# Attention and MLP in one launch: the order of loads and first steps in the opening

## The chip, the cores and the metric

The kernel runs on one core of one Trainium2 chip. The core has a matrix engine (TensorE, PE in the profile, with its weight loads shown apart as PEld), a vector engine (DVE), a scalar engine (ACT), a general engine (POOL) and SyncE (SP), which here issues every DMA transfer. Each engine works through its own list of instructions in the order in which they stand there, and waits where an operand or a buffer is not ready. The metric is the device time of one execution in microseconds (us). Times are compared as the median of several executions.

## The reference

The input x has 2048 tokens of width 512. It is normalised per token, and the normalised tokens go through an attention with 32 query heads that share one head of keys and values (head width 16), and through a two-layer MLP of width 1792 with the Mish activation. The output is x plus both results. Cut to what matters:

```python
xn = (x - mean(x)) / sqrt(var(x) + 1e-5)               # 2048 x 512
q  = (xn @ wq) split into 32 heads of 16
k, v = xn @ wk, xn @ wv                                # one head of 16 each
p  = softmax(q @ k.T * 16**-0.5)                       # 32 x 2048 x 2048
A  = (p @ v for all heads, joined) @ wo
h  = xn @ w1 + b1
B  = (h * tanh(softplus(h))) @ w2                      # Mish, width 1792
out = x + A + B
```

Everything is float32. Products are made with a split of each operand into a high part and the remainder, three terms of four, so every matrix needs a rounded copy (hi) and a difference (lo) before it is used.

## The kernel before, in words

The work has two parts. The **opening** (the block under `with tc.tile_pool(name="first", ...)`) takes some 100 us. It loads the tokens in four chunks of 512 (chunk c is four tiles of 128 tokens), normalises them, transposes them on PE, and projects them to keys, values and queries. It also makes the first two tiles of the MLP (`hidden(0)`, `hidden(1)`) and the row maxima of the scores of the first four heads. The **main part** then follows a long string, `PLAN`, that fixes the order of scores, exponentials, values, MLP products and loads, one letter per step. The change does not touch this string.

In the opening the order on every engine is the order in which the Python code issues instructions: nothing is reordered. Some instructions are put off with `later(...)` and issued by a `flush(...)` of their tag. The functions that matter here, with the names that the profile shows:

- `load_tokens(c)` issues four DMAs into tiles `pt` (L314). `statistics(c)` makes mean and variance of each tile on DVE (L322, L323). `rooted(c)` puts variance and mean into `v` and `m` (DVE, L329, L330) and has ACT make the first guess of 1/sqrt by Ln and Exp (L331, L332). `root(c, engine)` improves it by a Newton step (L337 to L340). `normalise` and `normalise_on_two` scale the tiles (DVE or POOL L346, ACT L354).
- `first_transposes` and `transposes` turn the tiles on PE (L361, L375); ACT copies the result out of PSUM as the hi part of `X` (L363, L377), and DVE or POOL subtract for the lo part (L387).
- `keys_values(c)` multiplies `X` by `wkv` (PE L412); ACT copies the result twice (L417, L418), and POOL makes 16 rows of differences in `KS`. `queries(c, mt)` and `hidden(f)` are generators whose 12 products are issued by `Piece.product` (PE L703) in portions, wherever the code calls `fill_slot`. ACT copies a query block out (L448, L449), POOL makes its lo part (L452), SP sends it on (L458 to L475).
- `query_block(mt)` and `request("w1", f, ...)` load weights into a raw tile (`raw_block`, L257); `split` makes hi on ACT (L240) and lo on POOL (L241). Raw tiles are a ring of three (`RAWS`), shared by the query blocks and the MLP's blocks.
- `first_maxima` makes scores of the first heads (PE L490) into a pair of banks and takes their maxima on DVE (L507).

PSUM has eight banks. Three pairs rotate (`pair_bank`), bank 6 is called `o`, bank 7 `misc`. The first MLP tile, the second one and the query blocks of chunk 0 all use bank 7:

```python
p = bank("o", f"q{c}_{mt}", 1) if beside == [] and turn[0] % 2 else misc(f"q{c}_{mt}")
p = misc(f"h0_{f}")
```

`beside` holds the transposes and projections of chunks 2 and 3 and becomes empty only after they have been issued, so until then a query block may begin only when ACT has copied out the tile that was in bank 7 before.

SP's list is one queue too. A load that waits for a raw tile holds back everything behind it, including the copies of the first query block into `QS` (L469), which the first scores need.

Of the kernel before, what the change touches and what calls it, by code (L numbers as in the profile page):

```python
# [17 lines left out]
P = 128  # L18
# [16 lines left out]
WARM = 54  # L35
# [143 lines left out]
def attention_and_mlp(ctx: ExitStack, tc: tile.TileContext, x, wq, wk, wv, wo, w1, b1, w2, out):  # L179
# [73 lines left out]
    def raw_block(kind, i):  # L253
        raw = work.tile([P, D], F32, tag="raw", name=f"raw_{kind}{i}", bufs=RAWS)
# [61 lines left out]
    def statistics(c, some=range(NT)):  # L316
# [7 lines left out]
        if len(some) == NT:  # L324
            rooted(c)

    def rooted(c):
        v, y, z, m = (first.tile([P, NT], F32, tag=n, name=f"{n}{c}", bufs=2) for n in ("v", "y", "z", "m"))
        DVE.tensor_scalar_add(v, MV[c][:, :, 1], EPS)  # L329
        DVE.tensor_scalar_mul(m, MV[c][:, :, 0], -1.0)  # L330
        ACT.activation(z, v, AF.Ln)  # L331
        ACT.activation(y, z, AF.Exp, scale=-0.5)  # L332
        ROOT[c] = v, y, z, m

    def root(c, engine):
        v, y, z, m = ROOT[c]
        engine.tensor_tensor(out=z, in0=y, in1=y, op=ALU.mult)  # L337
# [10 lines left out]
    def normalise_on_two(c, n):  # L348
        v, y, z, mean = ROOT[c]
        DVE.tensor_tensor(out=z, in0=y, in1=mean, op=ALU.mult)  # L350
        normalise(c, DVE, range(n))
# [298 lines left out]
    def hidden(f):  # L650
# [3 lines left out]
        p = misc(f"h0_{f}")  # L654
# [80 lines left out]
    with tc.tile_pool(name="first", bufs=1) as first:  # L735
# [6 lines left out]
        request("w1", 0, WB[0])  # L742
# [7 lines left out]
        SP.dma_start(out=b1s, in_=b1.rearrange("(f p) -> p f", p=P))  # L750
# [9 lines left out]
        wkv = first.tile([P, 2, DT, P], F32R, name="wkv")  # L760
        for r in (0, 64):
# [8 lines left out]
        statistics(0)  # L770
        request("w1", 1, WB[1])
        ask()
        root(0, DVE)
        normalise_on_two(0, 2)
        WQ[1] = query_block(1)
        load_tokens(2)
        for mt in range(2, DT):
            WQ[mt] = query_block(mt)
        load_tokens(3)
        urgent += [queries(*divmod(i, DT)) for i in range(1, NC * DT)]  # L780
        ask()
# [324 lines left out]
```

## Time and profile before

| | |
|---|---|
| Median of 3 runs | 1553.24 us (1551.15 to 3630.99) |
| Profiled execution, its time | 1553.4 us |
| Profiled execution, its span | 1551.4 us |
| Mean granted PE clock | 0.999 |
| PE busy, DVE, ACT, POOL | 1539.8, 1346.6, 1343.8, 862.9 us |
| First product of queries and keys of chunk 0 | 12.80 us |
| First scores of the first heads | 32.01 us |
| First scores of the main part | 100.40 us |

The run of 3630.99 us stands far from the other two, which are 2.1 us apart. The span runs from the first to the last instruction; the time has about 2 us around it. In rows of the timeline the two numbers ahead are the start and the length in us, then come engine, line, operation, output and inputs, the number of instructions that a row merges, and in square brackets how long the engine had stood idle before it and what ended that.

### The profile page before, as it was taken

How to read it: one execution, taken by the hardware profiler on the slowest of the kernel's cores; microseconds unless marked ns; L12 is line 12 of the kernel's file. 1: busy time of each engine (PE TensorE's matmuls, PEld its weight loads, DVE VectorE, ACT ScalarE, POOL GpSimd, SP SyncE). 2: the span in 40 equal slices, each digit the busy share in tenths (PEclk: the TensorE clock that was granted, in tenths of full speed). 3: DMA queues.
4: the chain of work that ended last, by engine and by line, in shares of the span. 5: the costliest groups of instructions: out<-in, count | busy, mean ns of one | idle time of the engine just before them, and what ended most of it. 6: DMA issues, size and time to landing. Idle time of an engine off the chain costs nothing.

```text
span 1551.4 us, 30232 instructions
## 1 busy us (share of the span) xinstructions
PE 1539.8 (99%) x11554; PEld 847.3 (55%) x11554; DVE 1346.6 (87%) x2284; ACT 1343.8 (87%) x2388; POOL 862.9 (56%) x757
## 2 busy tenths in 40 slices
PE   8999999999999999999999999999999999999998
PEld 6665554555555555555555545555555555555555
DVE  6869998898999898999889999999988998999841
ACT  5569988999999889898889888988898989888896
POOL 5768765676565546544554474833374746353652
PEclk9999999999999999999999999999999999999999
DMA  6783322242122321125322321132222222142120
GB/s 187 279 301 113 107 85 87 82 141 105 60 66 87 119 73 60 45 72 173 80 73 93 112 90 43 51 124 103 86 94 79 86 78 80 32 127 94 43 96 29
DMA packets 69399, 152.53 MB, mean 98 GB/s; under 512 B 12774, under 2 KB 22054, under 8 KB 68870
## 3 DMA queue, kind: packets, MB, share of 16 engines
q1 hardware_dynamic: 69254, 150.60, 29.8%
q8 instruction: 91, 1.49, 0.4%
q14 instruction: 54, 0.44, 0.1%
HBM read 98.51 MB, written 51.64 MB: 97 GB/s over the span
## 4 chain that ended last, share of the span: by engine, by line
PE 96%; DMA 1%; DVE 0%; ACT 0%; issue 0%; SPq 0%; POOL 0%; ACTq 0%; POOLq 0%; DVEq 0%
PE banks L560 32%; PE banks L934 24%; PE banks L556 18%; PE banks L490 18%; PE banks L703 3%; DMA ring<-w_dram 1%; PE banks L642 1%; PE banks L412 0%; DMA wkv_raw<-in_A_wv_dram 0%; DMA pt<-in_A_x_dram 0%; PE banks L375 0%; DVE ysb L632 0%; POOL wblk L241 0%; SPq L314 0%; DVE X L387 0%
## 5 line engine op out<-in xcount | busy, mean ns | idle before, releaser
L502 DVE TENSOR_REDUCE nm<-banks 128x1 f32<-128x512 f32 x1984 | 1241.1, 683 | 126.1 <-PE banks L490 75.9
L999 ACT ACTIVATE pt<-banks 128x512 f32<-128x512 f32 x1590 | 858.3, 604 | 105.6 <-PE banks L556 51.5
L490 PE MATMUL banks<-KS,QS 48*128 48x512 f32 x2048 | 694.6, 421 | 0.0
L556 PE MATMUL banks<-QS,KS 64*128 64x512 f32 x2048 | 681.5, 418 | 0.0
L560 PE MATMUL banks<-pt,V 128*32 128x512 f32 x4096 | 536.2, 603 | 0.0
L556 PEld LDWEIGHTS banks<-QS,KS 64*128 64x128 f32 x2048 | 330.9, 184 | 224.7 <-DVE nm L502 106.5
L490 PEld LDWEIGHTS banks<-KS,QS 48*128 48x128 f32 x2048 | 334.1, 185 | 195.7 <-DVE nm L502 99.8
L934 PE MATMUL banks<-X,wblk 64*128 64x512 f32 x1296 | 330.9, 396 | 0.5
L934 PE MATMUL banks<-ring,act 64*128 64x512 f32 x1344 | 328.4, 396 | 0.8 <-DMA ring<-w_dram 0.6
L991 ACT ACTIVATE pt<-banks 128x1024 f32<-128x1024 f32 x229 | 233.1, 1029 | 34.6 <-PE banks L556 21.0
L934 PEld LDWEIGHTS banks<-X,wblk 64*128 64x128 f32 x1296 | 215.1, 185 | 31.5 <-issue 15.4
L934 PEld LDWEIGHTS banks<-ring,act 64*128 64x128 f32 x1344 | 212.3, 185 | 36.4 <-issue 10.3
L560 PEld LDWEIGHTS banks<-pt,V 128*32 128x32 f32 x4096 | 85.8, 108 | 176.7 <-issue 166.0
L945 POOL TENSOR_TENSOR ysb<-ysb,ty 128x512 f32<-128x512 f32 x80 | 102.7, 1285 | 122.7 <-ACT ty L944 122.1
L683 POOL TENSOR_TENSOR tn<-tn,tr 128x512 f32<-128x512 f32 x54 | 69.3, 1284 | 139.1 <-ACT tr L1009 139.0
L1004 POOL TENSOR_SCALAR tu<-tu 128x512 f32<-128x512 f32 x54 | 80.3, 1487 | 119.1 <-ACT tu L1003 118.8
L241 POOL TENSOR_TENSOR act<-th,act 128x512 fp32r<-128x512 f32 x56 | 72.0, 1288 | 128.3 <-ACT act L240 106.9
L686 POOL TENSOR_TENSOR th<-th,tn 128x512 f32<-128x512 f32 x56 | 72.3, 1291 | 0.0
L685 POOL TENSOR_TENSOR tz<-tz,tn 128x512 f32<-128x512 f32 x54 | 69.5, 1287 | 4.5
L1006 POOL TENSOR_TENSOR tn<-tn,tu 128x512 f32<-128x512 f32 x54 | 69.5, 1287 | 4.5
L687 POOL TENSOR_TENSOR th<-th,tz 128x512 f32<-128x512 f32 x54 | 69.5, 1287 | 4.2
L934 PE MATMUL banks<-ring,ohl 64*128 64x512 f32 x288 | 65.5, 397 | 0.0
(116 smaller groups left out, 960.2 us busy)
## 6 DMA issues: line engine op xcount, KB each, us to landing
wblk<-w_dram SPq DMA_DIRECT2D x42, 512.0 KB
ring<-w_dram SPq DMA_DIRECT2D x42, 512.0 KB
QS<-q_dram SPq DMA_DIRECT2D x62, 192.0 KB
q_dram<-q SPq DMA_DIRECT2D x16, 512.0 KB
o_dram<-ov SPq DMA_DIRECT2D x31, 256.0 KB
raw_w<-in_B_w_dram SPq DMA_DIRECT2D x28, 256.0 KB
w_dram<-wblk SPq DMA_DIRECT2D x14, 512.0 KB
w_dram<-ring SPq DMA_DIRECT2D x14, 512.0 KB
```

Of the source, the lines that this page charges most:

```text
L241: POOL.tensor_tensor(out=lo, in0=src, in1=hi.bitcast(F32), op=ALU.subtract)
L490: PE.matmul(tile, QS[u][rows, pair, qt * P : (qt + 1) * P], KS[rows, kc * CT : (kc + 1) * CT], start=True, stop=True,)
L502: DVE.tensor_reduce(out=m[:, a : a + 1], in_=tile, axis=AX.X, op=ALU.max)
L556: PE.matmul(bank, KS[rows, kt * P : (kt + 1) * P], QS[u][rows, pair], start=True, stop=True)
L560: PE.matmul(BANK[7][h * 32 : (h + 1) * 32], V[:, kt], PT.pop((u * KT + kt) * HG + h), start=kt == 0, stop=kt == KT - 1,)
L685: POOL.tensor_tensor(out=z, in0=z, in1=n, op=ALU.subtract)
L686: POOL.tensor_tensor(out=h, in0=h, in1=n, op=ALU.mult)
L934: PE.matmul(self.p, w[rows], x[rows], start=self.first, stop=not any(self.todo))
L945: POOL.tensor_tensor(out=YS[t], in0=YS[t], in1=ty, op=ALU.add)
L991: ACT.activation(slots[slot // 2], banks[:, bank : bank + 2], AF.Exp, scale=SCALE)
L999: ACT.activation(PT[n], BANK[bank], AF.Exp, scale=SCALE)
L1004: POOL.tensor_scalar_min(tu, tu, U_MAX)
```

## The change

Six things are altered, all in the opening:

- The raw tiles of query blocks 1 to 3 are no longer taken from the ring of three. They lie in tiles that the MLP uses later (`TN[0]`, `TN[1]`, `TH[2]`; `tn` and `th` in the order below).
- All loads of the opening are issued at its beginning, in the order MLP block 0, bias, MLP block 1, chunk 2, query blocks 1 and 2, chunk 3, query block 3.
- The statistics, the root and the scaling of chunk 0 are done in two halves of two tiles; POOL makes the Newton step of the first half. The split of `wkv` is divided: keys ahead of the second half's root, values behind the scaling.
- The Newton step is one instruction shorter on DVE, and the bias of ACT's scaling is made only for ACT's columns.
- The first MLP tile goes to bank 6.
- Some steps of chunks 1 to 3 trade places: the second MLP block is split earlier, `rooted(2)` and chunk 1's lo parts come ahead of the statistics of chunk 3, and two of these move behind the first two maxima. PE's first 54 transposes of the identity become 44.

```diff
-WARM = 54
+WARM = 44
@@ raw_block
-        raw = work.tile([P, D], F32, tag="raw", name=f"raw_{kind}{i}", bufs=RAWS)
+        if kind == "wq" and i:
+            raw = (TN + TH[2:])[i - 1]
+        else:
+            raw = work.tile([P, D], F32, tag="raw", name=f"raw_{kind}{i}", bufs=RAWS)
@@ rooted, root
-        DVE.tensor_scalar_add(v, MV[c][:, :, 1], EPS)
+        DVE.tensor_scalar(v, MV[c][:, some, 1], EPS, -0.5, op0=ALU.add, op1=ALU.mult)
-        ACT.activation(z, v, AF.Ln)
+        ACT.activation(z, v, AF.Ln, scale=-2.0)
...
-        engine.tensor_scalar(z, z, -0.5, 1.5, op0=ALU.mult, op1=ALU.add)
-        engine.tensor_tensor(out=y, in0=y, in1=z, op=ALU.mult)
+        if engine is DVE:
+            DVE.scalar_tensor_tensor(out=y, in0=z, scalar=1.5, in1=y, op0=ALU.add, op1=ALU.mult)
+        else:
+            engine.tensor_scalar_add(z, z, 1.5)
+            engine.tensor_tensor(out=y, in0=y, in1=z, op=ALU.mult)
@@ first_transposes
-        for t in (0, 2, 1, 3):
+        for t in range(NT):
@@ hidden
-        p = misc(f"h0_{f}")
+        p = misc(f"h0_{f}") if f else bank("o", f"h0_{f}", 1)
@@ opening
         load_tokens(1)
-        request("w1", 0, WB[0])
+        for f in range(2):
+            request("w1", f, WB[f])
+            ask()
+            if f == 0:
+                SP.dma_start(out=b1s, in_=b1_column)
+        load_tokens(2)
+        for mt in range(1, DT - 1):
+            WQ[mt] = query_block(mt)
+        load_tokens(3)
+        WQ[DT - 1] = query_block(DT - 1)
...
+        statistics(0, range(2))
+        rooted(0, halves[0])
+        root(0, POOL, halves[0])
         for r in (0, 64):
             hi, lo = (wkv[:, i, :, r : r + 48].rearrange("p t (k d) -> p t k d", k=3) for i in range(2))
             split(hi, lo, wkv_raw[:, :, None, :DH].to_broadcast([P, DT, 3, DH]))
-            split(wkv[:, 0, :, r + 48 : r + 64], wkv[:, 1, :, r + 48 : r + 64], wkv_raw[:, :, DH:])
-        statistics(0)
...
+        statistics(0, range(2, NT))
+        rooted(0, halves[1])
+        normalise(0, DVE, range(2))
+        root(0, DVE, halves[1])
+        normalise_on_two(0, 3, 2)
+        for r in (0, 64):
+            split(wkv[:, 0, :, r + 48 : r + 64], wkv[:, 1, :, r + 48 : r + 64], wkv_raw[:, :, DH:])
...
+        split_block()
         statistics(1, range(2))
...
-        split_block()
         flush(("k", 0))
         flush(("wq", 1), ("wq", 2))
+        statistics(2)
         fill_slot(12)
         run(transposes(1))
-        flush(("wq", 3))
-        statistics(2)
+        rooted(2)
+        flush(("lo", 1))
         statistics(3, range(2))
-        flush(("lo", 1))
         fill_slot(12)
         root(2, POOL)
         normalise(2, POOL)
-        statistics(3, range(2, NT))
         run(keys_values(1))
+        flush(("wq", 3))
...
             if i == 1:
+                statistics(3, range(2, NT))
                 rooted(3)
```

How this moves instructions is seen best engine by engine. On SP, the stretch between the second MLP block and the copies of the first query block reads before (`pt_82`, `pt_83` are the tiles of chunk 2, `pt_84`, `pt_85` those of chunk 3, two tiles each; the brackets name the semaphores waited for):

```order
L257 DMA raw_w_205<-in_B_w_dram 128x4x128 [waits DMAHW5_49]
L257 DMA raw_wq_217<-in_A_wq_dram 128x4x128 [waits DMAHW6_49,Pool_49]
L314 DMA pt_82<-in_A_x_dram 128x512 [waits DMAHW7_49]
...
L257 DMA raw_wq_224<-in_A_wq_dram 128x4x128 [waits DMAHW3_49,Pool_49]
L257 DMA raw_wq_227<-in_A_wq_dram 128x4x128 [waits DMAHW5_49,DMAHW4_49,Pool_49]
L314 DMA pt_84<-in_A_x_dram 128x512
...
L469 DMA QS_88<-q_0_307 16x2x512 [waits DMAHW1_49]
```

and after:

```order
L260 DMA raw_w_113<-in_B_w_dram 128x4x128 [waits DMAHW5_49]
L317 DMA pt_82<-in_A_x_dram 128x512 [waits DMAHW6_49]
...
L260 DMA tn_76<-in_A_wq_dram 128x4x128 [waits DMAHW2_49]
L260 DMA tn_77<-in_A_wq_dram 128x4x128 [waits DMAHW3_49]
L317 DMA pt_84<-in_A_x_dram 128x512 [waits DMAHW4_49]
...
L260 DMA th_75<-in_A_wq_dram 128x4x128 [waits DMAHW0_49]
L474 DMA QS_88<-q_0_303 16x2x512 [waits DMAHW1_49,Activation_49]
```

(Three dots stand for the chunk's other tiles.) The three loads of query blocks waited for POOL to release a raw tile, and wait now only for earlier transfers.

On DVE, from the last values of chunk 2 to the root of chunk 3, before (`st_398` are the statistics of chunk 3, `X_357` is the transposed chunk 1, `nm` the maxima):

```order
L330 TENSOR_SCALAR m_393<-mv_381 128x4
L322 BN_STATS st_398<-pt_84 128x6
L323 BN_AGGR mv_399<-st_398 128x2
...
L387 TENSOR_TENSOR X_357<-banks,X_357 128x1024 x2
L322 BN_STATS st_398<-pt_85 128x6
L323 BN_AGGR mv_399<-st_398 128x2
...
L507 TENSOR_REDUCE nm_451<-banks 128x2 x2
L329 TENSOR_SCALAR v_460<-mv_399 128x4
```

and after (`X_360` is the transposed chunk 1, `st_389` the statistics of chunk 3):

```order
L333 TENSOR_SCALAR m_382<-mv_335 128x4
L392 TENSOR_TENSOR X_360<-banks,X_360 128x1024 x2
L325 BN_STATS st_389<-pt_84 128x6
L326 BN_AGGR mv_390<-st_389 128x2
...
L512 TENSOR_REDUCE nm_440<-banks 128x2 x2
L325 BN_STATS st_389<-pt_85 128x6
L326 BN_AGGR mv_390<-st_389 128x2
...
L332 TENSOR_SCALAR v_453<-mv_390 128x4
```

The lo parts of chunk 1 moved ahead of the first two statistics of chunk 3, and the first two maxima ahead of the other two. (Where three dots stand, the same rows follow for the next tile of the chunk.) On ACT the copy of query block 1 out of PSUM stands behind Ln and Exp of chunk 3's root in both kernels; after the change these rows read:

```order
L423 ACTIVATE KS<-kvs_431 128x512
L240 ACTIVATE wq_127<-th_75 128x256 x2
L334 ACTIVATE z_455<-v_453 128x4
L335 ACTIVATE y_454<-z_455 128x4
L453 ACTIVATE q_1_473<-banks 128x512
```

Here the split of query block 3 has moved in from an earlier place on ACT; the three rows below it stand as before.

More of the change, by code (lines that the diff above doesn't have):

```diff
@@ L323, in statistics, with rooted, root @@
             DVE.bn_aggr(out=MV[c][:, t], in_=st[:, t])
[L324 to L328, printed above, removed]
[L329 to L331 removed]
+    def rooted(c, some=slice(0, NT)):
+        if c not in ROOT:
+            ROOT[c] = [first.tile([P, NT], F32, tag=n, name=f"{n}{c}", bufs=2) for n in ("v", "y", "z", "m")]
+        v, y, z, m = (t[:, some] for t in ROOT[c])
+        DVE.tensor_scalar(v, MV[c][:, some, 1], EPS, -0.5, op0=ALU.add, op1=ALU.mult)
+        DVE.tensor_scalar_mul(m, MV[c][:, some, 0], -1.0)
+        ACT.activation(z, v, AF.Ln, scale=-2.0)
         ACT.activation(y, z, AF.Exp, scale=-0.5)
[L333 to L336 removed]
+    def root(c, engine, some=slice(0, NT)):
+        v, y, z, m = (t[:, some] for t in ROOT[c])
         engine.tensor_tensor(out=z, in0=y, in1=y, op=ALU.mult)
         engine.tensor_tensor(out=z, in0=z, in1=v, op=ALU.mult)
[L339 to L340 removed]
+        if engine is DVE:
[3 more added lines that the diff above has]
+            engine.tensor_tensor(out=y, in0=y, in1=z, op=ALU.mult)
     def normalise(c, engine, some=range(NT)):
@@ L346, in normalise, with normalise_on_two @@
             engine.tensor_scalar(x, x, m, r, op0=ALU.add, op1=ALU.mult)
-    def normalise_on_two(c, n):
+    def normalise_on_two(c, n, begin=0):
         v, y, z, mean = ROOT[c]
-        DVE.tensor_tensor(out=z, in0=y, in1=mean, op=ALU.mult)
-        normalise(c, DVE, range(n))
+        DVE.tensor_tensor(out=z[:, n:], in0=y[:, n:], in1=mean[:, n:], op=ALU.mult)
+        normalise(c, DVE, range(begin, n))
         for t in range(n, NT):
@@ L768, in run @@
                 pass
-        statistics(0)
[L771 to L781, printed above, removed]
         flush(("wq", 0))
```

4 lines of the change are left out of this document (3 added, 1 removed).

## The prediction

> **What bounds the kernel now.** I read the page's totals and chain first.
>
> ```profile
> PE 1539.8 (99%) x11554; PEld 847.3 (55%) x11554; DVE 1346.6 (87%) x2284; ACT 1343.8 (87%) x2388; POOL 862.9 (56%) x757
> PE 96%; DMA 1%; DVE 0%; ACT 0%; issue 0%; SPq 0%; POOL 0%; ACTq 0%; POOLq 0%; DVEq 0%
> ```
>
> PE is the bound, and its list behind the opening is untouched. So the change is worth what it moves PE's list forward by the end of the opening, and that carries to the end undiminished. Next I read PE's timeline over the opening:
>
> ```profile
> 1.35 7.73 PE L747 MATMUL banks<-ident 128*128 128x128 f32 x54 [1.35 <-POOL ident masks.py:199]
> 12.80 0.73 PE L412 MATMUL banks<-X,wkv 128*128 128x512 f32 x2 [0.33 <-ACT X L363]
> 13.37 0.63 PE L703 MATMUL banks<-X,wq 128*128 128x512 f32 x2
> ...
> 17.55 1.08 PE L703 MATMUL banks<-X,wq 128*128 128x512 f32 x4
> 19.61 3.02 PE L703 MATMUL banks<-X,wblk 128*128 128x512 f32 x12 [0.98 <-ACT q L448]
> 22.47 2.08 PE L375 MATMUL banks<-ident,pt 128*128 128x128 f32 x16
> 24.31 3.01 PE L703 MATMUL banks<-X,wblk 128*128 128x512 f32 x12
> 27.16 2.00 PE L412 MATMUL banks<-X,wkv 128*128 128x512 f32 x8
> 30.23 0.73 PE L412 MATMUL banks<-X,wkv 128*128 128x512 f32 x2 [1.07 <-DVE X L387]
> 31.36 0.72 PE L412 MATMUL banks<-X,wkv 128*128 128x512 f32 x2 [0.40 <-DVE X L387]
> 32.01 1.22 PE L490 MATMUL banks<-KS,QS 48*128 48x512 f32 x4
> 33.17 4.08 PE L703 MATMUL banks<-X,wq 128*128 128x512 f32 x12
> 37.18 0.73 PE L490 MATMUL banks<-KS,QS 48*128 48x512 f32 x4
> 37.84 0.75 PE L375 MATMUL banks<-ident,pt 128*128 128x128 f32 x4
> 38.35 1.43 PE L703 MATMUL banks<-X,wq 128*128 128x512 f32 x5
> ```
>
> Three things stand out: PE waits at 19.6 for ACT's copy of query block 0, it waits at 29 to 31.4 for chunk 1's lo parts, and 12 products that take 2.85 us at 24.31 (to the next row) take 4.0 us at 33.17. The stretches by half microseconds explain the last one (the column behind POOL is the granted clock):
>
> ```profile
> 32.00:32.50 0.50, 0.50 (x3) 0.49 (x4) 0.50 (x2) 0.38 (x1) 0.50 (x1) 0.52 1.02 381
> 35.00:35.50 0.50, 0.50 (x3) 0.37 (x2) 0.49 (x3) 0.04 (x1) 0.44 (x2) 0.57 0.30 33
> ```
>
> The shares 0.52 and 0.57 put its ends at 32.02 and 35.43: the clock was halved for 3.41 us, right behind the gaps.
>
> **The change part by part.** *Front (chunk 0).* The rows of its chain:
>
> ```profile
> 3.43 0.69 DVE L322 BATCH_NORM_STATS2 st<-pt 128x6 f32<-128x512 f32 x1 [2.58 <-DMA pt<-in_A_x_dram]
> 7.67 0.66 ACT L240 ACTIVATE wkv<-wkv_raw 128x64 fp32r<-128x64 f32 x3 [0.97 <-DMA wkv_raw<-in_A_wv_dram]
> 8.00 1.16 POOL L241 TENSOR_TENSOR wkv<-wkv_raw,wkv 128x64 fp32r<-128x64 f32 x3 [0.64 <-ACT wkv L240]
> 9.69 1.00 DVE L346 TENSOR_SCALAR pt<-pt,m,y 128x512 f32<-128x512 f32 x2
> 9.81 1.52 ACT L354 ACTIVATE pt<-pt,z,y 128x512 f32<-128x512 f32 x2 [1.16 <-DVE z L350]
> 10.97 1.45 POOL L387 TENSOR_TENSOR wq<-raw_wq,wq 128x256 fp32r<-128x256 f32 x2 [1.82 <-DVE wq L291]
> 12.15 2.07 ACT X L363 x4
> 29.87 0.20 POOL L337 TENSOR_TENSOR z<-y 128x4 f32<-128x4 f32 x1
> ```
>
> Two tiles' statistics (0.83 each with the aggregate) end at 5.15, `v` and `m` at 5.5, Ln and Exp at 5.85. POOL's four small steps (0.20 each, some 0.28 apart) end at 6.95, when DVE is still at tiles 2 and 3; it has their `v` and `m` at 7.6, scales tiles 0 and 1 by 8.6, makes the second root (three steps and the bias, 0.25 each) by 9.55, tile 2 by 10.05. ACT scales tile 3 (0.76) by 10.3. Its copies of `X` can begin at 10.9 in place of 12.15: 1.25 us. But the value columns of `wkv` now stand behind that scaling: ACT 2 x 0.22, POOL 2 x 0.39, and behind them on POOL query block 0's lo part, 1.45, ends at 12.85. PE's fourth product needs it and starts at 12.95; before, it started at 13.37 + 0.23 = 13.60. I take this later wait, **0.65**; ends 0 (a small step held up) and 1.25. The ten transposes left out end PE's warming at about 8.3 in place of 9.08, ahead of the first scaled tile's transposes, so they are worth nothing by themselves.
>
> *Bank 6 for the first MLP tile.* The four products at 17.55 end their streaming at 18.48; with no wait for ACT's copy the next follow at once instead of at 19.61: **1.13**. Cover: the block's lo part was done on POOL at 16.1, and is at 14.95 now. The tokens of chunk 1 come next; ACT's scaling of the last one moves by the front's 0.65 to 20.3, PE reaches them at 20.7. Ends 0.7 and 1.13. Bank 6 is wanted again by chunk 1's keys, 25.4, and ACT empties it by 22.3.
>
> *Loads and chunk 1's lo parts.* Who kept DVE waiting, and why the data were late:
>
> ```profile
> 16.14 7.29 SPq L257 DMA_DIRECT2D raw_wq<-in_A_wq_dram  x2
> 23.48 2.04 SPq L314 DMA_DIRECT2D pt<-in_A_x_dram  x4
> 25.56 3.91 SPq L469 DMA_DIRECT2D QS<-q  x6
> SPq L257 <- POOL wblk L241: 7.1, 2, 6.1
> 26.60 0.70 DVE L322 BATCH_NORM_STATS2 st<-pt 128x6 f32<-128x512 f32 x1 [2.29 <-DMA pt<-in_A_x_dram]
> 28.98 2.32 DVE L387 TENSOR_TENSOR X<-banks,X 128x1024 fp32r<-128x1024 f32 x2
> ```
>
> SP stood 6.1 us at query block 3's load, behind it chunk 3's loads, behind these on DVE the lo parts. Now the raw tiles are free and the lo parts come first: ACT, from its scaling's end at 20.3, has four splits of query blocks (0.34 each), the first MLP tile's copy (0.69) and two copies of chunk 1's hi parts (1.0 each), which end at 23.3 and 24.3; DVE, some 1.1 us earlier with chunk 1's scaling (19.1), is through chunk 2's four statistics at 22.9; the lo parts (1.16 each) are there at 24.5 and 25.7. PE wants them from 27.2 on. Eight products of 0.232 from 27.16 and four more would have ended at 29.95; the scores began at 32.01: **2.06**, both gaps go. What could be late in their place is data:
>
> ```profile
> 7.99 3.51 SPq L257 DMA_DIRECT2D raw_w<-in_B_w_dram  x1
> 11.50:12.00 0.50, 0.50 (x7) 0.50 (x6) 0.47 (x3) 0.00 (x0) 0.50 (x2) 1.00 0.26 2
> 24.00:26.00 2.00, 2.00 (x12) 1.71 (x12) 0.31 (x2) 1.71 (x3) 1.85 (x3) 1.00 0.87 264
> 26.00:28.00 2.00, 2.00 (x10) 1.66 (x9) 0.88 (x2) 1.58 (x5) 2.00 (x4) 1.00 1.02 319
> ```
>
> The second MLP block held SP until 11.5, and the DMA engines are all but idle then (last columns: share and GB/s), so it has landed; its split, now ahead of chunk 1's root on ACT, starts at 13.6 and waits for nothing. The ten tiles behind it, 2.6 MB, need 8 to 10 us at 264 to 319 GB/s: until 20 to 22, in order of need (chunk 2 about 15, wanted at 19.1; blocks 1 and 2 about 17, wanted at 20.2; chunk 3 about 20, wanted at 25.6). SP is free for the `QS` copies when POOL has the query's lo part, 20.9. They take 3.9 us to issue and then at most 2.5 us (29.47 to 32.0 before), so 27.3; PE wants them at 28.1. It holds by 0.8.
>
> *Clock.* Four scores and 12 products took 5.17 us from 32.01 to 37.18; by the rows at full clock (0.66 from 37.18, 2.85 from 24.31) they take 3.51: **1.66** if closing the gaps keeps the clock. Ends 0 and 1.66.
>
> *A new wait.* Query block 2 needs bank 7, so ACT's copy of query block 1, which stands behind Ln and Exp of chunk 3's root; that root now waits on DVE behind two maxima and two statistics. Rows:
>
> ```profile
> 32.88 2.36 DVE L507 TENSOR_REDUCE nm<-banks 128x2 f32<-128x1024 f32 x2
> 37.28 0.60 ACT L448 ACTIVATE q<-banks 128x512 f32<-128x512 f32 x1 [1.39 <-PE banks L703]
> ```
>
> From the first score: 0.54 to the maximum (37.18 to 37.72 in DVE's next such row), 2.36, 2 x 0.83, `v` 0.2, Ln and Exp 0.48, the copy 0.60: 5.84. PE is there after 0.66 + 2.85 + 0.66 + 0.51 = 4.68. **-1.16**. Before, the statistics were ahead of the maxima and the slow clock gave time, so ACT even waited 1.39 for PE. Ends -1.2 and 0. POOL's list is 3.5 to 4 us ahead at chunk 2's scaling (30.5; PE transposes at 32.3), so it is not what is late.
>
> Sum: 0.65 + 1.13 + 2.06 + 1.66 - 1.16 = 4.3 us. From the profiled execution's 1553.4 this leaves **1549.0**; that execution is 0.2 from the median, 1553.24, so the same number stands for the median.
>
> **A rule on the clock.** The Trainium skill, page "TensorE: Matmul & The Clock Gate", section "HAM oscillation — how this bites in real kernels", asks for PE-idle gaps over some 3.4 us before the clock falls. By that rule the 1.66 would not be earned by closing gaps of 1.2 and 0.4, and the sum would be 2.7, so 1550.7. The trace speaks against it: the fall came right behind a stretch of 3.41 us (28.61 to 32.02) in which PE was busy for about 1.9. The page's section on the clock gate says that the window runs freely, which the 3.41 us here agree with.
>
> **Rivals.** *The half clock comes anyway, in another place.* The changed front has gaps too (9.3 to 10.1, between the transposes of tiles 1 and 2, and most of 11.2 to 12.95): a stretch of 3.4 us from 9.3 holds about 1.8 of work, no more than the one that lost the clock; one from 8.1 holds 2.2, as the stretch from 8.14 before, which kept it. It depends on where the window falls. Price 1.7: 1550.7. **25%**. *No new wait at query block 2* (the maxima begin earlier, or front and bank give more): 1547.5. **12%**. *The change does not do what it says:* the data or copies are late by some of what was saved, or the gain is taken back by a wait between 40 and 100 us; the opening's end moves 0 to 2: 1552.3. **7%**. *Slower: the prefetch holds back the first query's copies.* All ten loads now stand ahead of them. If SP is held as at 7.99 and the transfers run at the 150 GB/s of the row from 10 to 12, 2.6 MB end at 29, the copies land at 29 + 3.9 + 2.5 = 35.4 in place of 28.1: 7.3 lost, 1556. It decides against the change when the mean rate is under 2.6 MB in (21 + 4.3 - 11.5) us, 190 GB/s; rows with a full queue show 264 and more. **4%**.
>
> ```profile
> 10.00:12.00 2.00, 1.71 (x14) 1.71 (x15) 1.97 (x7) 1.33 (x2) 1.03 (x2) 1.00 0.98 150
> ```
>
> **How the numbers follow.** The forecast, 1549.0, has 52%. The two undisturbed runs before lie 2.1 us apart, so each case is some 1 us wide on either side. Low end: forecast with no new wait and the front's 1.25, 1547.2, less 0.7 for that spread: 1546.5. High end: the half clock and no gain in front, 1551.4, and 1.6 towards the failing case: 1553.0. All cases lie within 1% of 1553.24, and 2% is 31 us, about what a measurement of this kernel can tell from no change. A third of the opening would have to be lost or won to leave that band: faster 1%, within 98%, slower 1%.
>
> **What would show it.** First MLP product about 17.9 instead of 19.61 without a wait; no idle ahead of chunk 1's four last products; scores from about 28.1; clock 1.00 there; a wait of about 1.1 for ACT's copy ahead of query block 2; the main part's first scores at 96.1 instead of 100.40. A half clock elsewhere, `QS` copies that PE waits for, or main-part scores that start at 100 would make it wrong.

## The result

The changed kernel takes 1549.78 us in the median (1548.28 to 1551.77), the kernel before 1552.93 us beside it. The ratio is 0.9982, interval 0.9974 to 0.9991: 3.2 us less, far inside 2%. The profiled execution of the changed kernel took 1549.18 us, its span is 1547.3 us, 4.1 less than before, and the mean granted clock is 1.00.

The page's totals and its chain of waits, changed kernel:

```profile
PE 1537.1 (99%) x11544; PEld 844.9 (55%) x11544; DVE 1348.7 (87%) x2285; ACT 1342.8 (87%) x2389; POOL 865.0 (56%) x761
PE 97%; DVE 2%; ACT 0%; DMA 0%; issue 0%; SPq 0%; ACTq 0%; DVEq 0%
```

PE bounds the kernel as it did. The 1% of DMA that stood in the chain is gone. The timeline of PE over the opening (start, length, engine, line, operation, operands; in brackets the idle time before it and what ended that):

```profile
11.52 0.73 PE L417 MATMUL banks<-X,wkv 128*128 128x512 f32 x2 [0.33 <-ACT X L368]
12.09 0.99 PE L708 MATMUL banks<-X,wq 128*128 128x512 f32 x2
...
17.56 2.90 PE L708 MATMUL banks<-X,wblk 128*128 128x512 f32 x12
...
24.98 2.91 PE L417 MATMUL banks<-X,wkv 128*128 128x512 f32 x12
27.81 0.92 PE L495 MATMUL banks<-KS,QS 48*128 48x512 f32 x4
28.66 3.01 PE L708 MATMUL banks<-X,wq 128*128 128x512 f32 x12
31.61 0.73 PE L495 MATMUL banks<-KS,QS 48*128 48x512 f32 x4
...
34.38 1.43 PE L708 MATMUL banks<-X,wq 128*128 128x512 f32 x5 [1.37 <-ACT q L453]
...
96.76 0.50 PE L495 MATMUL banks<-KS,QS 48*128 48x512 f32 x1
```

The waits at 19.6 (first MLP product) and at 29 to 31.4 (keys of chunk 1) are gone, and a new one of 1.37 us stands ahead of query block 2. The lead over before grows and shrinks along this list:

| point | before | after | lead | step |
|---|---|---|---|---|
| fourth product | 13.60 | 12.69 | 0.91 | +0.91 |
| first MLP product | 19.61 | 17.56 | 2.05 | +1.13 |
| keys of chunk 1 | 27.16 | 24.98 | 2.18 | +0.13 |
| first scores | 32.01 | 27.81 | 4.20 | +2.02 |
| second scores | 37.18 | 31.61 | 5.57 | +1.37 |
| query block 2 | 38.35 | 34.38 | 3.97 | -1.60 |
| main part | 100.33 | 96.76 | 3.57 | -0.40 |

(The fourth product is the second of the row at 12.09: that row's end less one product's 0.39. The main part of before is taken from its timeline's row, 100.33, where the table ahead of the change has 100.40.) The granted clock is full where it had been 0.52 and 0.57, in stretches of the changed kernel (after the length: busy time and count of PE, weight loads, DVE, ACT, POOL; then clock, DMA share, GB/s):

```profile
28.50:32.00 3.50, 3.50 (x18) 2.47 (x16) 3.47 (x6) 1.29 (x4) 3.50 (x5) 1.00 0.07 20
32.00:35.50 3.50, 2.13 (x13) 1.50 (x10) 3.43 (x6) 2.03 (x6) 2.89 (x3) 1.00 0.19 59
```

The new wait is read from the other engines' rows:

```profile
28.54 2.36 DVE L512 TENSOR_REDUCE nm<-banks 128x2 f32<-128x1024 f32 x2
30.81 0.68 DVE L325 BATCH_NORM_STATS2 st<-pt 128x6 f32<-128x512 f32 x1
32.08 2.59 POOL L392 TENSOR_TENSOR KS<-kvs,KS 16x512 fp32r<-16x512 f32 x2
32.54 0.83 DVE L332 TENSOR_SCALAR v<-mv 128x4 f32<-128x4 f32 x1
33.40 0.20 ACT L334 ACTIVATE z<-v 128x4 f32<-128x4 f32 x1 [3.58 <-DVE v L332]
33.75 0.58 ACT L453 ACTIVATE q<-banks 128x512 f32<-128x512 f32 x1
```

ACT does nothing for 3.58 us because Ln of chunk 3's root waits for DVE's `v`, and the copy that PE wants stands behind it. `v` itself takes 0.83 us for 128x4 numbers and ends at 33.37; the first of POOL's two subtractions, which began before it, ends at 32.08 + 1.30 = 33.38.

Some data came later than the prediction had it, with nothing lost on PE:

```profile
14.52 0.63 ACT L240 ACTIVATE wblk<-raw_w 128x512 fp32r<-128x512 f32 x1 [1.07 <-DMA raw_w<-in_B_w_dram]
22.34 0.75 ACT L240 ACTIVATE wq<-tn 128x256 fp32r<-128x256 f32 x2 [1.63 <-DMA tn<-in_A_wq_dram]
```

### The profile page after: what moved, and what is told of

Read it like the earlier page. It is cut to its first block, busy times and chain, and to the rows that moved or that the text cites. A ratio compares the mean times of both kernels' runs of the same rounds, so it can differ in the third digit from the quotient of the medians.

```text
span 1547.3 us, 30218 instructions
## 1 busy us (share of the span) xinstructions
PE 1537.1 (99%) x11544; PEld 844.9 (55%) x11544; DVE 1348.7 (87%) x2285; ACT 1342.8 (87%) x2389; POOL 865.0 (56%) x761
## 4 chain that ended last, share of the span: by engine, by line
PE 97%; DVE 2%; ACT 0%; DMA 0%; issue 0%; SPq 0%; ACTq 0%; DVEq 0%
PE banks L565 33%; PE banks L948 24%; PE banks L561 19%; PE banks L495 18%; PE banks L708 3%; PE banks L647 1%; DVE st L325 0%; PE banks L417 0%; DVE nm L507 0%; DVE X L392 0%; DMA pt<-in_A_x_dram 0%; PE banks L380 0%; DVE pt L351 0%; DVE v L332 0%; DVE ysb L637 0%; DVE nm L512 0%
```

## The experiments

The profiled executions differ by up to 1.2 us in when the third token tile's statistics begin on DVE, mostly because of when its data arrive. So small differences between kernels are counted from there (5.49 in the changed kernel). In this table the times behind the first column are counted from there; the span is that of the profiled execution. The count is steady for the kernels with the changed front (5.98 to 6.21 for the first product). With one root for all of chunk 0 it leans on other things too, such as when the weights land: 7.40 in before, 7.12 and 7.13 in y_filler and y_order, 6.74 in y_loads, where the third tile was late. Differences of that size between the two kinds of front are not read from it.

| kernel | third tile | first product of keys | first scores | main part | span |
|---|---|---|---|---|---|
| before | 5.40 | 7.40 | 26.61 | 94.93 | 1551.4 |
| changed | 5.49 | 6.03 | 22.32 | 91.27 | 1547.3 |
| x_bank7 | 5.86 | 6.04 | 23.53 | 91.70 | 1548.3 |
| x_order | 6.19 | 6.08 | 22.51 | 91.21 | 1547.4 |
| x_front | 5.94 | 6.43 | 22.35 | 91.25 | 1548.8 |
| y_loads | 6.29 | 6.74 | 23.91 | 91.05 | 1547.8 |
| y_order | 5.34 | 7.13 | 26.50 | 95.25 | 1551.4 |
| y_filler | 5.09 | 7.12 | 26.34 | 93.13 | 1550.2 |
| z_copy_first | 5.87 | 5.98 | 22.27 | 89.49 | 1545.9 |
| z_later | 5.49 | 6.21 | 22.51 | 91.65 | 1547.0 |
| w_no_scalar | 6.06 | 6.04 | 22.32 | 90.91 | 1548.3 |

### One part of the change undone

**x_bank7**: the first MLP tile goes back to bank 7.

```diff
-        p = misc(f"h0_{f}") if f else bank("o", f"h0_{f}", 1)
+        p = misc(f"h0_{f}")
```

> The changed kernel with the first MLP tile back in bank 7; nothing else differs. If the bank is worth what the sum gave it, PE's first MLP product starts when ACT has copied query block 0, at 18.7 us in place of 17.56, with a wait of about 1.1, and the main part's first scores stand at 97.9 in place of 96.76 (span about 1548.4). The rival, that the transposes of chunk 1 would wait for their tokens anyway, gives the same late MLP product but first scores of the main part at 97.0 or earlier.

PE's timeline, x_bank7:

```profile
19.01 3.02 PE L708 MATMUL banks<-X,wblk 128*128 128x512 f32 x12 [0.92 <-ACT q L453]
35.15 1.43 PE L708 MATMUL banks<-X,wq 128*128 128x512 f32 x5 [0.74 <-ACT q L453]
```

The wait for bank 7 is back, and the first scores come 1.21 us later than in the changed kernel (23.53 against 22.32). The main part comes only 0.43 later: the wait ahead of query block 2 shrank from 1.37 to 0.74. So the free bank wins about 1.1 on the spot, and about 0.8 of it is given back at block 2. The main part at 97.56 (97.2 without the 0.37 by which the third tile came later) lies between the two expectations.

**x_order**: chunk 1's lo parts go behind the first two statistics of chunk 3 again.

```diff
-        flush(("lo", 1))
         statistics(3, range(2))
+        flush(("lo", 1))
```

> The changed kernel with chunk 1's lo parts on DVE again behind the first two statistics of chunk 3. Theory: the early loads removed the gap ahead of chunk 1's last products and the order is spare: chunk 3 has landed by then, the two statistics take 1.7 us, the first scores begin at 27.8 to 28.4 in place of 27.81, the clock stays at 1.00, and the main part's first scores stand within 0.6 us of 96.76. Rival, the order did it: a gap of 1 to 2 us returns, with or without the half clock, and the main part begins at 98 to 100.

PE's products of chunk 1's keys, x_order:

```profile
25.73 3.03 PE L417 MATMUL banks<-X,wkv 128*128 128x512 f32 x12
```

No gap, full clock, the main part as in the changed kernel. With the data there, the order of these steps is spare.

**x_front**: chunk 0's statistics, root and scaling in one go. The order of the first transposes and the undivided split of `wkv` go back with them; the 44 transposes of the identity, the shorter Newton step and the smaller bias stay.

```diff
-        statistics(0, range(2))
-        rooted(0, halves[0])
-        root(0, POOL, halves[0])
...
+        statistics(0)
+        rooted(0)
+        root(0, DVE)
+        normalise_on_two(0, 2)
```

> The changed kernel with chunk 0 normalised in one go as before (statistics, root and scaling of four tiles together, both parts of the weights of keys and values split ahead of them). Theory: PE's products of keys and queries begin 1.0 to 1.3 us later but their fourth only 0.9 later, since it no longer waits for query block 0's lo part; everything behind moves by 0.9 and the main part begins at 97.7 in place of 96.76, give or take 0.4 for when the first tokens arrive. Rival: some of it is hidden behind chunk 1's loads or tokens, and the main part begins at 97.0 or earlier.

PE's first products, x_front, and ACT's split of the key weights:

```profile
12.37 0.73 PE L417 MATMUL banks<-X,wkv 128*128 128x512 f32 x2 [0.33 <-ACT X L368]
6.77 0.91 ACT L240 ACTIVATE wkv<-wkv_raw 128x192 fp32r<-128x192 f32 x4 [1.80 <-DMA wkv_raw<-in_A_wk_dram]
```

The main part begins at 97.19, between the two expectations; counted from the third tile it stands where the changed kernel's does, which is the rival's case. The first product of keys is 0.40 later by the table (6.43 against 6.03), but the fourth product stands at 13.17 (a row at 12.93 of 0.63, less 0.39), 7.23 from the third tile against 7.20 in the changed kernel, and the scores stand where they stood. In the changed kernel the fourth product waits for POOL's lo part of query block 0 (the row at 12.09 takes 0.99 for two products of 0.39 and 0.23), and this takes back what the halves win ahead of it. So in this execution the halves won nothing of the front's 0.91. It is one execution, and its third tile came 0.45 later than the changed kernel's; with early tokens the halves could win some, which is not shown. In before, ACT had stood at the landing of the value weights until 7.67 (the row that the prediction shows), with Ln behind it; in x_front the weights had landed together.

### One part of the change alone

**y_loads**: the kernel before with the raw tiles and the early loads, nothing else. Its lines are numbered a little otherwise.

```diff
+        if kind == "wq" and i:
+            raw = (TN + TH[2:])[i - 1]
...
+        for f in range(2):
+            request("w1", f, WB[f])
+            ask()
...
+        load_tokens(2)
+        for mt in range(1, DT - 1):
+            WQ[mt] = query_block(mt)
+        load_tokens(3)
+        WQ[DT - 1] = query_block(DT - 1)
```

> The kernel before with one part of the change alone: all loads early and the raw tiles of query blocks 1 to 3 in tiles of the MLP; every engine but SP keeps its order. Theory: chunk 3's tokens and the copies of the first query are early, so DVE makes chunk 1's lo parts from about 26 to 28.4, PE has no gap, the first scores begin at 29.9 to 30.0 in place of 32.01, the clock stays at 1.00, and the main part begins at about 96.9 (2.0 for the gap, 1.4 to 1.7 for the clock off 100.33). Rival, the order on DVE is needed: first scores at 31 or later and the main part at 99 or later.

PE's timeline, y_loads:

```profile
19.83 3.02 PE L706 MATMUL banks<-X,wblk 128*128 128x512 f32 x12 [0.96 <-ACT q L451]
27.37 2.91 PE L415 MATMUL banks<-X,wkv 128*128 128x512 f32 x12
30.20 0.73 PE L493 MATMUL banks<-KS,QS 48*128 48x512 f32 x4
34.98 1.41 PE L706 MATMUL banks<-X,wq 128*128 128x512 f32 x5
```

The gaps of chunk 1's keys are gone with the old order of statistics, the clock stays full, and no wait stands ahead of query block 2. The main part begins 91.05 after the third tile's start, no later than in the whole change (91.27). What front and bank win in the whole change (scores 1.6 earlier) is lost again by the main part.

**y_order**: the kernel before with chunk 1's lo parts ahead of the first two statistics of chunk 3.

```diff
         statistics(2)
-        statistics(3, range(2))
         flush(("lo", 1))
+        statistics(3, range(2))
```

> The kernel before with another part alone: chunk 1's lo parts on DVE ahead of the first two statistics of chunk 3; loads as before. Theory: the lo parts come in time and chunk 1's products end at 29.95, but the copies of the first query, issued from 25.6 to 29.5, are not there yet, so PE waits at the first scores instead until 30.5 to 32; the main part begins at 98.5 to 100.3, the later end if the clock is halved all the same. Rival, the order suffices: first scores at 29.95, main part at 96.9.

PE's timeline, y_order, and a stretch of it by engines:

```profile
26.82 2.91 PE L412 MATMUL banks<-X,wkv 128*128 128x512 f32 x12
31.84 1.29 PE L490 MATMUL banks<-KS,QS 48*128 48x512 f32 x4 [2.12 <-DMA QS<-q]
```

```profile
32.00:36.00 4.00, 3.96 (x11) 2.65 (x11) 3.23 (x5) 0.41 (x2) 3.86 (x5) 0.60 0.37 134
```

The gaps inside the keys close, and a wait of 2.12 us for the copies into `QS` takes their place: these stand behind the same late loads on SP. The clock is halved here too. So the late loads were behind the gaps, and the order wins nothing alone.

**y_filler**: the kernel before with 12 and 6 transposes of the identity in the two gaps of chunk 1's keys; PE does more work, none of it used.

```diff
+            if c == 1 and n in (8, 10):
+                for i in range(12 if n == 8 else 6):
+                    PE.transpose(banks[:, 0, i % NT * P : (i % NT + 1) * P], ident, ident)
             PE.matmul(p, w, x, start=n == 0, stop=n + 1 == len(products))
```

> The kernel before with 18 transposes of the identity into a free pair of banks, 12 ahead of chunk 1's ninth key product and 6 ahead of the eleventh, which stand in the two gaps (1.07 and 0.40 us) in which PE waits for chunk 1's lo parts. They compute nothing that is used. If the clock falls because PE does too little in a stretch of 3.4 us, it stays at 1.00 through 40 us, the first scores begin where they did (within 0.3 of 32.0, counted from the same front), four scores and 12 products take 3.5 to 3.8 us in place of 5.17, and the main part begins 1.4 to 1.7 us earlier. If the fall has nothing to do with the gap (the rule that only idle gaps over some 3.4 us count, or a window of its own), a half clock of 3.41 us appears here too and nothing is won.

PE's timeline, y_filler, and the same stretch:

```profile
28.44 1.47 PE L414 MATMUL banks<-ident 128*128 128x128 f32 x12
31.43 0.73 PE L493 MATMUL banks<-KS,QS 48*128 48x512 f32 x4
32.09 3.06 PE L706 MATMUL banks<-X,wq 128*128 128x512 f32 x12
```

```profile
32.00:36.00 4.00, 4.00 (x20) 2.73 (x19) 3.31 (x5) 1.80 (x6) 3.86 (x4) 1.00 0.12 28
```

The scores come when they came (19.22 from the first product of keys, 19.21 before), but four scores and 12 products take 3.65 us in place of 5.17. The clock stays at 1.00, and the main part is 1.5 us earlier from the first product of keys (86.01 against 87.53). This fits the expectation that PE's idle time in that stretch was what cost the clock. It does not prove it: it is one execution, and in the section on times 11 of 26 executions of the kernel before kept the full clock with no filling at all. The filling also closes the gaps and raises the busy share at once, so it would not tell which of the two counts. A step of this size is not to be seen in the single times (1552.05 us against 1552.57 for before beside it).

### The new wait

**z_copy_first**: the changed kernel with the products of query block 1, and with them ACT's copy, issued ahead of the rest of chunk 3's statistics and root.

```diff
             if i == 1:
+                fill_slots(12)
                 statistics(3, range(2, NT))
                 rooted(3)
...
-            if i == 1:
-                fill_slots(12)
```

> The changed kernel with one trade on ACT: the copy of query block 1 out of PSUM ahead of Ln and Exp of chunk 3's root; DVE, PE and POOL keep their order. If the wait of 1.37 us at query block 2 comes from that order, it goes; chunk 2's copies still stand behind Ln and Exp, and the third maximum behind chunk 3's values on DVE, so PE gives back some 0.4 before its next transposes. Main part at about 95.7 in place of 96.76. Rival: the bank is not what holds block 2, and a wait of over 1 us stays.

PE's, ACT's, DVE's and POOL's rows, z_copy_first:

```profile
31.86 0.60 ACT L453 ACTIVATE q<-banks 128x512 f32<-128x512 f32 x1 [1.71 <-PE banks L708]
32.72 0.17 DVE L332 TENSOR_SCALAR v<-mv 128x4 f32<-128x4 f32 x1
32.79 2.66 POOL L392 TENSOR_TENSOR KS<-kvs,KS 16x512 fp32r<-16x512 f32 x2
32.92 1.41 PE L708 MATMUL banks<-X,wq 128*128 128x512 f32 x5
```

No wait ahead of query block 2: ACT now waits for PE. The main part is 1.78 us earlier than in the changed kernel (89.49 against 91.27), and the wait was 1.37. `v` began 0.07 ahead of POOL's subtraction here, and took 0.17. The same kernel was profiled a second time (t_copy_first, below), and there POOL began first:

```profile
32.02 2.60 POOL L392 TENSOR_TENSOR KS<-kvs,KS 16x512 fp32r<-16x512 f32 x2
32.44 0.87 DVE L332 TENSOR_SCALAR v<-mv 128x4 f32<-128x4 f32 x1
34.56 0.75 PE L380 MATMUL banks<-ident,pt 128*128 128x128 f32 x4 [0.47 <-DVE nm L512]
```

`v` took 0.87, the maximum behind it came later, and PE waited 0.47 us for it ahead of its next transposes, about the 0.4 that the expectation allowed for. So whether `v` or POOL's subtraction begins first can differ between two executions of one kernel.

**z_later**: the order of the changed kernel, but the rest of chunk 3's statistics one portion later, its root two.

```diff
-            if i == 1:
+            if i == 3:
                 statistics(3, range(2, NT))
+            if i == 5:
                 rooted(3)
```

> The changed kernel with the last two statistics of chunk 3 behind the fourth maximum on DVE, and its values, Ln and Exp behind the sixth, so nothing of chunk 3 stands between the first maxima and the copies of query block 1 and chunk 2. The wait at query block 2 goes altogether: main part at about 95.3 in place of 96.76, span some 1.4 below the changed kernel's. Rival: chunk 3's root comes too late for its transposes and part of it returns after 45 us.

PE's and ACT's rows, z_later:

```profile
38.65 0.20 ACT L334 ACTIVATE z<-v 128x4 f32<-128x4 f32 x1 [2.83 <-DVE v L332]
40.61 1.65 PE L708 MATMUL banks<-X,wq 128*128 128x512 f32 x6 [2.46 <-ACT q L453]
```

The wait left block 2 and stands ahead of block 3, 2.46 us long, for the same reason: Ln is again ahead of the copies on ACT. The main part gains nothing (91.65), and the expectation did not hold. In these two runs it counts whether ACT's list has a step that waits for DVE ahead of a copy that PE wants, not how late that step is issued.

**w_no_scalar**: the changed kernel with `v` and `m` computed by another operation of DVE.

```diff
-        DVE.tensor_scalar(v, MV[c][:, some, 1], EPS, -0.5, op0=ALU.add, op1=ALU.mult)
+        DVE.scalar_tensor_tensor(out=v, in0=MV[c][:, some, 1], scalar=EPS, in1=HALF[0][:, some], op0=ALU.add, op1=ALU.mult)
```

> Changed kernel, with the two small DVE steps of each chunk's root (`v` and `m`, 128x4) written as SCALAR_TENSOR_TENSOR with a tile that holds -0.5, in place of TENSOR_SCALAR; nothing else moves. In the changed kernel `v` took 0.56, 0.83 and 1.05 us in chunks 1 to 3, and ended each time within 0.03 us of the end of a POOL TENSOR_TENSOR that ran beside it. Theory (a TENSOR_SCALAR on small tiles in memory is held until POOL's running instruction ends, another operation of DVE is not): `v` takes about 0.15 to 0.2 us in every chunk, ends ahead of POOL's instruction where one runs beside it, the wait ahead of query block 2 falls from 1.37 us to about 0.7 and the scores behind it from 37.14 to about 36.5 (counted from the third tile's arrival, 31.65 to about 31.0). Rival (the end beside POOL's was chance, or any small DVE operation in memory is slow beside POOL): `v` keeps 0.5 to 1.1 us, and the wait keeps 1.37.

DVE's and POOL's rows, w_no_scalar:

```profile
21.28 2.65 POOL L392 TENSOR_TENSOR KS<-kvs,KS 16x512 fp32r<-16x512 f32 x2
22.61 0.17 DVE L332 SCALAR_TENSOR_TENSOR v<-mv,half 128x4 f32<-128x4 f32 x1
22.69 1.26 DVE L333 SCALAR_TENSOR_TENSOR m<-mv,half 128x4 f32<-128x4 f32 x1
32.55 2.60 POOL L392 TENSOR_TENSOR KS<-kvs,KS 16x512 fp32r<-16x512 f32 x2
32.73 0.18 DVE L326 BATCH_NORM_AGGREGATE mv<-st 128x2 f32<-128x6 f32 x1
32.95 0.90 DVE L332 SCALAR_TENSOR_TENSOR v<-mv,half 128x4 f32<-128x4 f32 x1
34.87 1.43 PE L708 MATMUL banks<-X,wq 128*128 128x512 f32 x5 [1.47 <-ACT q L453]
```

The theory as worded fell: the other operation is held as well. `v` takes 0.90 in chunk 3 and ends at 33.85, and so does POOL's first subtraction (32.55 + 1.30); the wait stays, at 1.47. But not every small step on DVE is slow beside POOL, as the rival had it: the aggregate at 32.73 takes 0.18 while the same subtraction runs.

### Times

Three kernels on one chip beside the kernel before (1552.42 us median): z_copy_first, y_loads and the changed kernel again.

> The changed kernel with the copy of query block 1 ahead of Ln and Exp of chunk 3's root, timed in five rounds. One look gave a main part that begins 1.4 us earlier than the changed kernel's (95.36 against 96.76). If that carries to the end, its time is 1.4 us under the changed kernel's on the same chip, some 4.5 to 5 under the kernel before: ratio 0.997. Rival: a shift this small in the opening is lost in the rest, and both kernels have the same ratio within 0.0003.

> The kernel before with the early loads alone, timed in five rounds. One look gave a span of 1547.8 against 1547.3 of the whole change. If the loads are the change, as its opening says, its ratio to the kernel before is 0.9975 to 0.9985, the same as that of the whole change within 0.0005. Rival: the other parts add a microsecond that one look did not show, and the ratio is 0.9987 or more.

> The changed kernel again, in five rounds on the chip of the two others, so that the three can be compared: ratio to the kernel before 0.9974 to 0.9991 as first measured; 1.4 us above the kernel with query block 1's copy first, and within 1 us of the one with the early loads alone.

| kernel | median, us | ratio to before | main part begins |
|---|---|---|---|
| t_copy_first | 1548.34 (1546.97 to 1548.81) | 0.9973 (0.9962 to 0.9983) | 95.78 |
| t_loads | 1549.69 (1548.59 to 1550.26) | 0.9985 (0.9976 to 0.9993) | 96.80 |
| t_after | 1549.38 (1547.88 to 1551.32) | 0.9984 (0.9975 to 0.9992) | 96.60 |

Within what these times can tell, the loads alone are worth what the whole change is worth. With the copy first, 4.1 us are gone, a little less than the 4.5 to 5 expected; the interval overlaps that of the changed kernel, so the 1.0 us between them rests on the traces (the main part begins 0.82 earlier here, 1.40 in the first pair) more than on the times.

Each of these executions also has a mean granted clock. One half clock of 3.41 us lowers it by 0.001 (before, profiled: 0.999), so 1.000 means that there was none of that length. It was 1.000 in only 11 of the 26 executions of the kernel before, whose median is 1550.83 us; the other 15 have 1553.34. It was 1.000 in all 12 of t_loads, in 8 of 11 of t_after (median 1549.20) and in 7 of 8 of t_copy_first. So the kernel before does not lose the clock every time. The early loads alone go with a full clock in every execution, which is the stronger evidence that they keep it. Where the kernel before keeps it too, the whole change is worth some 1.6 us (1550.83 against 1549.20). A mean of 0.999 does not say that time was lost: in z_later the clock falls only in the last 2 us of the span, where PE has nothing left to do.

## Why the prediction was right

The forecast of 1549.0 stands beside 1549.78 in the median and 1549.18 in the profiled execution, and in the trace the case that was given the 52% is the one that came: both gaps closed, full clock, a new wait at query block 2. The places and the chain of the wait were read rightly. That the sum came out so near is partly luck: some terms did not come from where the prediction had them, and their errors cancel in part. By its terms:

- **Front, 0.65 predicted, 0.91 measured.** The fourth product does wait for query block 0's lo part on POOL, as the prediction had it. But the nearness of the size is luck: x_front has the gain without the halves. What made the profiled execution of before late was in part when its weights landed, which the prediction read as fixed; in y_order and y_filler, with the same front, the first product came 0.27 and 0.28 earlier by the table. Nor are the ten transposes left out worth nothing each time: in y_filler and t_loads the 54 end only at 9.95 and 10.20, and the first tile's transposes follow at 9.79 and 10.04 without a wait for the tile, which DVE had ready at about 9.3 to 9.4 (its rows of two tiles begin at 8.79 and 8.83 and take 1.00).
- **Bank 6, 1.13 and 1.13.** The term held at its place. The prediction took it as carried to the end; x_bank7 shows 0.43 of it there, because the new wait grows by most of what PE gains.
- **Loads and lo parts, 2.06 and 2.02.** Both gaps went. The prediction gave the reorder a share; x_order, y_loads and y_order show that the loads do it and the order is spare.
- **Clock, 1.66 and 1.37.** Full clock through the stretch, as forecast where the gaps close; t_loads has it in 12 of 12 executions. The size is off by the two durations it was worked out from. The four scores take 0.85 in this execution (27.81 to 28.66), but 0.66 or 0.67 in t_after and in every other kernel at full clock, as the prediction had it. The 12 products take 2.95 (28.66 to 31.61) and 2.94 to 2.99 in the others, where the prediction had 2.85 from a row with no scores behind it. In t_after both together take 3.66, which makes the term 1.51. And the term can only be won where the kernel before loses the clock, in at most 15 of its 26 timed executions.
- **New wait, -1.16 and -1.60 of lead, 1.37 in the row.** The place and the chain were right: Ln behind `v` behind two maxima and two statistics. The term was mis-sized in one step, "`v` 0.2": it took 0.83, and 0.63 more is what POOL's running subtraction held it. The trace of before had shown the same in chunk 2, where `v` ends at 24.24 and the first of POOL's two subtractions, halfway through its row, at 24.25:

```profile
22.93 2.65 POOL L387 TENSOR_TENSOR KS<-kvs,KS 16x512 fp32r<-16x512 f32 x2
23.52 0.72 DVE L329 TENSOR_SCALAR v<-mv 128x4 f32<-128x4 f32 x1
```

- **Nothing later: -0.40.** The prediction let the lead carry undiminished. From the last four of the first scores to the main part, before, y_order and y_filler need 17.97 to 17.98 us, and the kernels with the early loads 18.34 or 18.35, all but w_no_scalar, which needs 18.06. The 0.36 lies in the 75 products of that stretch (17.75 us against 17.38 in their row, at a clock of 1.00). It comes with the loads in all kernels but that one; what takes it is open.

Together the terms give 3.57 at the main part, 0.77 short of the 4.34 that they were to sum to. The new wait and the last stretch cost 0.84 more than allowed, and the clock and the loads gave 0.33 less; the front gave 0.26 more, and 0.13 came between the MLP's products and the keys. The profiled span fell by 4.1 all the same, because the main part, whose list is the same, took 0.5 less in this execution (1450.54 against 1451.07 from its first scores to the end). That this execution ends 0.2 from the forecast is therefore luck; the medians, 3.2 apart, lie nearer to the terms. The sum also gave the parts other than loads and clock 0.62 in all (0.65 + 1.13 - 1.16), and by y_loads and t_loads, which do without them, they are worth next to nothing at the main part.

Wrong, but hidden: the data. The prediction had query blocks 1 and 2 landing about 17 and the second MLP block's split waiting for nothing. ACT waited 1.07 us for the one until 14.5 and 1.63 for query block 2 until 22.3 (the rows above). A mean rate from rows with a full queue was too fast for this stretch. Eleven loads stand ahead of the copies into `QS`, too, not ten (query block 3's is among them). PE did not wait for ACT then, and no wait of PE for the copies into `QS`, issued from 19.37 on, stands in the trace, so the rival by which the prefetch delays them did not come. Nor did the case without a new wait, which in the changed kernel needs an edit (z_copy_first). A half clock elsewhere did not come in the profiled execution; in five of the ten timed ones the mean granted clock is 0.998 or 0.999, and without a trace it stays open whether that cost time.

On the clock, the rule from the Trainium skill by which the fall would need an idle gap of 3.4 us is not what the traces show: the clock fell behind gaps of 1.07 and 0.40 us in before and behind one of 2.12 us in y_order. The same page, "TensorE: Matmul & The Clock Gate", has a section "A second HAM failure mode: psum-queue depth-cycling" in which frequent short idle times between groups of products make the clock go up and down; that is nearer to the traces, which show one fall and one return in the opening.

## What to carry to other kernels

When a wait on the bounding engine is taken away, look for the next thing that is late at the same buffer; here 1.6 of 5.6 us were given back at one copy that stood behind a step of another chain in ACT's list. Put a step that waits for another engine behind the copies that free a bank, not ahead of them. Of several edits made together, run each alone: two of the six here, the free raw tiles and the early loads, carry nearly all of the gain.

## What the runs showed of the hardware

Rows of the changed kernel in which DVE's small step runs beside POOL, chunks 1 and 2 (the third is shown with the new wait):

```profile
15.23 1.30 POOL L241 TENSOR_TENSOR wblk<-raw_w,wblk 128x512 fp32r<-128x512 f32 x1 [0.41 <-ACT wblk L240]
15.99 0.56 DVE L332 TENSOR_SCALAR v<-mv 128x4 f32<-128x4 f32 x1
20.80 2.65 POOL L392 TENSOR_TENSOR KS<-kvs,KS 16x512 fp32r<-16x512 f32 x2
22.43 1.05 DVE L332 TENSOR_SCALAR v<-mv 128x4 f32<-128x4 f32 x1
```

- **A small step on DVE can be held until a POOL instruction ends.** In the changed kernel `v` took 0.56, 1.05 and 0.83 us in chunks 1 to 3. It ended at 16.55, 23.48 and 33.37, and a POOL subtraction that was already running at 16.53, 23.45 and 33.38; where it began first, it took 0.17 (z_copy_first). In w_no_scalar `v` at 22.61 slips in between two POOL instructions with 0.17 and `m` behind it takes 1.26, to the end of the second. Statistics beside POOL are not held (0.68 at 30.81 in the changed kernel, beside the split of query block 3; 0.18 at 32.73 in w_no_scalar). The Trainium skill, page "SBUF — State Buffer", section "SBUF: two separate sides", says that DVE and GpSimd (POOL) share one pair of ports, which an operation holds alone for its whole length, and that on DVE's side the operations that want it are those in a two-port mode and those with two inputs in SBUF. The rows here agree: w_no_scalar's replacement has two such inputs, and TENSOR_SCALAR fits if it runs in a two-port mode, which the trace does not show. That the ports are the cause is the page's statement; the runs show the coinciding ends.
- **The clock can fall without a long gap, but not each time.** In before PE was busy for about 1.9 of the 3.41 us ahead of the fall, with no wait longer than about 1.1 us, and the half clock then lasted 3.41 us too. In y_order one wait of 2.12 us did the same. In z_later a wait of 2.46 us did not (clock 1.00 in the row below), and 11 of 26 executions of the kernel before had no fall. All of this fits the prediction's remark that it depends on where the window falls; no run here shows it apart.

```profile
38.00:42.00 4.00, 1.54 (x8) 1.05 (x6) 0.69 (x3) 3.28 (x8) 1.87 (x2) 1.00 0.32 112
```

- **Transposes of the identity alone bring PE to full pace, and the clock column does not show the start.** In before the profile counts 16 of the first 54 in the 3.4 us from 1.3 and 32 in the 3.3 us from 4.7, when PE has nothing else to do, while the granted clock reads 1.00 in both stretches. When the pace doubles differs between executions (24 in the second stretch in y_filler, 22 in t_loads).
